# Attention keys stored block by block, constants in one transfer, stores spread over six blocks: a one-core attention and experts kernel

## The chip, the cores and the metric

The kernel runs on one core of a Trainium2 chip. The metric is the device time of one execution in microseconds (us); the number quoted for a kernel is the median of several runs. TensorE is called PE, its weight loads PEld, VectorE DVE, ScalarE ACT, GpSimd POOL and SyncE SP. SP does no arithmetic here: its queue issues nearly all transfers between the device's main memory and the on-chip memory. Those transfers are carried by 16 DMA engines.

## What is computed

Three layers follow each other. Attention has 8 heads over 4 sequences of 576 tokens; the first four heads see the last 32 keys, the other four see every fourth of the last 128. Its output, 2304 rows of 512, goes into a layer of 8 experts, of which each row uses the one with the highest gate value, and then into a plain feed-forward layer with a squared ReLU.

```python
scores = scale * np.matmul(q, k.transpose(0, 1, 3, 2))
mask_plain = (rel >= 0) & (rel < window)
mask_dil = (rel >= 0) & (rel < window * dilation) & (rel % dilation == 0)
...
attn = attn / (np.sum(attn, axis=-1, keepdims=True) + 1e-09)
return np.matmul(attn, v).astype(np.float32)
...
logits = x @ w_gate
e_idx = np.argmax(logits, axis=1)
...
eom = 1.0 / (1.0 + np.exp(-(x @ w_output_gate)))
for e in range(E):
    mask = e_idx == e
    h = np.maximum(x[mask] @ w1[e], 0.0)
    ye = h @ w2[e]
    out[mask] = gate_w[mask, None] * eom[mask, e, None] * ye
...
h = np.maximum(x @ w_in, 0.0)
return (h * h @ w_out).astype(np.float32)
```

## The kernel before

The 2304 tokens are cut into 18 blocks of 128. The attention stage is a loop over blocks 0 to 14 (`EARLY` is 15), written out by hand and software-pipelined: turn i transposes the probabilities of block i (`tr`), forms the scores of block i+2 (`qk`, L423 to L436), transposes the output of block i-1 (`xt`) and multiplies block i's probabilities by its values (`pv`). After the loop come blocks 15 to 17 with the last two groups of routing, and with them the start of the experts: once the most frequent expert is known (`choose`, its number in `e0_t`, L205), its first weights are loaded (`load_w(0, 0)`, L722), its list of tokens (`meta_load`, L723), and its rows are gathered from main memory (`gather(0)`, L725), where the attention stage has stored them in `x_d`. `gather(0)` reads rows of blocks 0 to 14 and so waits until all of these are stored. The first expert matrix product is L820.

Keys, queries and values are loaded in turn by SP. `load_k(i, n)` (L349) brings the keys of n blocks with two transfers into a ring of five blocks plus one that repeats the fifth for the wrap (`wrap`, L354). Before, the tile `kz` holds the four pairs of heads one after the other and within a pair the blocks, so a row of a load comes in four pieces of 512 bytes times n. `load_q` (L342) and `load_v` (L360) bring two blocks each, with rows of 4096 and 8320 bytes. `load_consts` (L401) issues six small transfers in turn 0, ahead of the values of blocks 4 and 5. `clear` (L411) sets the experts' lists in main memory to an empty mark in turn 3, with four transfers of 128 rows of 640 bytes.

`store(a, 2)` (L508) writes two blocks of attention output to `x_d` with three transfers: one for the 256 columns of the plain heads (L512), and one for each block's other 256 columns (L514), whose rows are put in another order on the way. `STORES` (L35) says in which turn a pair is stored: pairs 0 and 2 in turn 12, 4 to 8 in turn 13, 10 and 12 in turn 14; block 14 follows after the loop (L700).

The order of each engine's instructions is the order in which the program writes them. SP works through its queue in that order, so an instruction that waits holds up all behind it. Two kinds of waits matter: for an engine to be done with a buffer that a load overwrites, and for one of eight semaphores that SP's transfers use in turn, so that a transfer waits until the eighth before it has landed.

Of the kernel before, what the change touches and what calls it, by code (L numbers as in the profile page):

```python
# [10 lines left out]
F32 = mybir.dt.float32  # L11
F32R = mybir.dt.float32r
BF16 = mybir.dt.bfloat16
I32 = mybir.dt.int32
# [8 lines left out]
B, H, S, D = 4, 8, 576, 64  # L23
P = 128
NT = B * S
NB = NT // P

LAP = 5
# [15 lines left out]
MS = NT + 256  # L44
# [10 lines left out]
VL = -(-2 * VN // 128) * 128  # L55
VR = 6


# [8 lines left out]
@with_exitstack  # L67
def attention_experts_kernel(ctx: ExitStack, tc: tile.TileContext, qB, kB, vB, wg, wE, wF, consts, rows, ids, out):
    nc = tc.nc
# [14 lines left out]
    ones = cpool.tile([P, P], BF16, name="ones")  # L84
    w8 = cpool.tile([P, 4, E], F32, name="w8")
    eoff = cpool.tile([P, 4, E], F32, name="eoff")
    idsb = cpool.tile([P, NG, 4, 4], I32, name="idsb")
    wg_sb = cpool.tile([P, 4, 32], F32, name="wg_sb")
    cum = cpool.tile([P, NG + 1, E], BF16, name="cum")
# [233 lines left out]
    def attention():  # L323
# [6 lines left out]
        masks = c2.tile([P, 4, 2, 64], F32, name="masks")  # L330
        tri32 = c2.tile([P, P], F32, name="tri32")
        kz = c2.tile([P, 2, 4, (LAP + 1) * P], F32, name="kz")
        vb = c2.tile([P, 2, VR, 4, 4, D + 1], F32, name="vb")
# [15 lines left out]
        def load_k(i, n, engine=nc.sync):  # L349
            t = i % LAP  # L350
            for h2 in range(2):
                engine.dma_start(out=kz[h2:P:2, h2, :, P * (t + 1):P * (t + 1 + n)], in_=kB[h2, :, :, P * i:P * (i + n)])

        def wrap():  # L354

            o = LAP * P
            nc.scalar.copy(out=kz[:, :, 0:2, 96:P], in_=kz[:, :, 0:2, o + 96:o + P])
            nc.scalar.copy(out=kz[:, :, 2:4, 0:P], in_=kz[:, :, 2:4, o:o + P])

# [8 lines left out]
        def clear_k(t, first, second):  # L368
            first.memset(kz[:, 0, :, P * t:P * t + P], 0.0)
            second.memset(kz[:, 1, :, P * t:P * t + P], 0.0)  # L370

# [6 lines left out]
        o = 2 * P  # L378
# [3 lines left out]
        warm(8)  # L382
        nc.vector.memset(kz[:, :, 0:2, 96:P], 0.0)
        nc.vector.memset(kz[:, :, 2:4, 0:P], 0.0)
        load_q(1, 1)
# [15 lines left out]
        def load_consts():  # L401
            nc.sync.dma_start(out=wg_sb, in_=wg)
            nc.sync.dma_start(out=tri32, in_=consts[:, P:2 * P])
            nc.sync.dma_start(out=w8.rearrange("p a e -> p (a e)"), in_=consts[:, o + 512:o + 544])
            nc.sync.dma_start(out=eoff.rearrange("p a e -> p (a e)"), in_=consts[:, o + 544:o + 576])
            nc.sync.dma_start(out=idsb.rearrange("p a b c -> p (a b c)"), in_=ids)
            nc.sync.dma_start(out=rowc, in_=rows)

        z = stg.tile([P, DM], F32, tag="xg", name="zm", bufs=4).bitcast(I32)[:, 0:MS * E * 4 // P // 4].rearrange("p (n c) -> p n c", c=4)

        def clear():  # L411
            for h in range(4):
                nc.sync.dma_start(out=meta_d[E * MS // 4 * h:E * MS // 4 * (h + 1)].rearrange("(p n) c -> p n c", p=P), in_=z)

# [8 lines left out]
        def qk_mm(i):  # L423
            t = i % LAP
            s = ps_s.tile([P, H, 64], F32, tag="s", name="s")
            q = q_t.pop(i)
            for p in range(4):
                for c in range(4):
                    if p < 2:
                        rhs = kz[:, :, p, P * (t + 1) + 32 * (c - 1):P * (t + 1) + 32 * (c + 1)]  # L430
                    else:
                        rhs = kz[:, :, p, P * t:P * (t + 2)].rearrange("p h (s c m) -> p h s c m", s=2, c=4)[:, :, :, c, :]
                    nc.tensor.matmul(
                        out=s[32 * c:32 * c + 32, 2 * p:2 * p + 2, :], lhsT=q[:, p, 32 * c:32 * c + 32], rhs=rhs, start=True, stop=True
                    )
            s_t[i] = s  # L436
# [212 lines left out]
        for i in range(EARLY):  # L649
# [3 lines left out]
            t = (i + 2) % LAP  # L653
# [6 lines left out]

            for a in STORES.get(i, ()):
                store(a, 2)
            if i % 2 == 0 and i + 6 < NB:
# [866 lines left out]
def _layout(inputs):  # L1530
# [22 lines left out]
    kd = dilated(k, 0, 32).reshape(NB, 2, 2, P, D).transpose(2, 4, 1, 0, 3).reshape(2, D, 2, NT)  # L1553
    kB = np.ascontiguousarray(np.concatenate([kp, kd], axis=2))
    one = np.concatenate([v, np.ones((H, NT, 1), f)], axis=2)
# [18 lines left out]
def _consts():  # L1574
# [21 lines left out]
    rows = np.concatenate([e, E - 1 - e, np.array(WIN, f), e * MS, lt.reshape(-1), np.arange(NSPILL, dtype=f)])[None]  # L1596
    return dict(consts=consts, rows=np.ascontiguousarray(rows), ids=np.ascontiguousarray(ids.reshape(P, -1)))

# [13 lines left out]
```

## Time and profile before

| what | value |
|---|---|
| median of 3 runs | 741.49 us (737.64 to 742.68) |
| the profiled execution | 742.68 us, its span 741.0 us |
| PE busy | 698.2 us, 94% of the span |
| DVE, ACT, POOL busy | 487.4, 327.2, 115.0 us |
| DMA | 136.90 MB, 185 GB/s on average |

The span begins with the first instruction that the profile shows and ends with the last; 1.7 us of the execution lie around it. The profiled execution is the slowest of the three, 1.2 us above the median. Up to about 110 us PE is idle a good part of the time; from about 125 us on it is busy nearly without a break. In the rows below "[idle before <-releaser]" is how long the engine sat idle ahead of the instruction and what ended that.

### The profile page before, as it was taken

How to read it: one execution, taken by the hardware profiler on the slowest of the kernel's cores; microseconds unless marked ns; L12 is line 12 of the kernel's file. 1: busy time of each engine (PE TensorE's matmuls, PEld its weight loads, DVE VectorE, ACT ScalarE, POOL GpSimd, SP SyncE). 2: the span in 40 equal slices, each digit the busy share in tenths (PEclk: the TensorE clock that was granted, in tenths of full speed). 3: DMA queues.
4: the chain of work that ended last, by engine and by line, in shares of the span. 5: the costliest groups of instructions: out<-in, count | busy, mean ns of one | idle time of the engine just before them, and what ended most of it. 6: DMA issues, size and time to landing. Idle time of an engine off the chain costs nothing. (4 is left out here: it accounts for less than half of the span.)

```text
span 741.0 us, 13894 instructions
## 1 busy us (share of the span) xinstructions
PE 698.2 (94%) x5227; PEld 633.4 (85%) x5227; DVE 487.4 (66%) x898; ACT 327.2 (44%) x601; POOL 115.0 (16%) x122
## 2 busy tenths in 40 slices
PE   6699748999999999999999999999999999999995
PEld 4566527999999999999999999999988888888884
DVE  7656644587465665687886977877889854445431
ACT  2334323464454555565655555556444431222120
POOL 6244423510101101004400000000000030003003
PEclk9999987999999999999999999999999999999998
DMA  8988464766547567675437555466565453325302
GB/s 265 318 253 249 154 186 156 216 207 227 191 152 225 189 194 249 211 221 167 161 134 256 188 192 199 139 238 231 192 218 183 150 166 113 106 95 182 100 29 88
DMA packets 67155, 136.90 MB, mean 185 GB/s; under 512 B 10857, under 2 KB 43498, under 8 KB 66058
## 3 DMA queue, kind: packets, MB, share of 16 engines
q1 hardware_dynamic: 57434, 120.09, 50.4%
q0 software_dynamic: 4176, 10.57, 4.2%
q10 hardware_dynamic: 5472, 5.29, 2.1%
q8 instruction: 43, 0.70, 0.4%
q14 instruction: 30, 0.25, 0.1%
HBM read 102.00 MB, written 33.96 MB: 183 GB/s over the span
## 5 line engine op out<-in xcount | busy, mean ns | idle before, releaser
L1386 DVE TENSOR_TENSOR slot_d<-gq,slot_d 128x768 fp32r<-128x768 f32 x48 | 45.9, 957 | 64.3 <-ACT slot_d L1384 63.3
L1384 ACT CAST slot_d<-gq 128x768 fp32r<-128x768 f32 x48 | 40.0, 835 | 97.7 <-PE op L1422 86.9
L1431 POOL DMA_INDIRECT out<-os,idc x18 | 19.8, 1099 | 353.2 <-DVE os L1430 348.3
L834 ACT ACTIVATE hh<-hp 128x240 fp32r<-128x240 f32 (+6 forms) x72 | 29.1, 407 | 40.1 <-PE hp L822 39.7
L159 POOL DMA_INDIRECT xg<-x_d,mt x23 | 24.7, 1074 | 141.6 <-PE xp L183 95.8
L1377 DVE SCALAR_TENSOR_TENSOR gq<-gq 128x768 f32<-128x768 f32 x48 | 45.6, 950 | 1.0 <-DMA gq<-g_d 1.0
L1421 PE MATMUL op<-slot_b,slot_d 128*128 128x512 f32 x108 | 42.0, 389 | 0.0
L1423 PE MATMUL op<-slot_a,slot_d 128*128 128x512 f32 x108 | 42.0, 389 | 0.0
L1422 PE MATMUL op<-slot_b,slot_d 128*128 128x512 f32 x108 | 42.0, 389 | 0.0
L1423 PE MATMUL op<-slot_b,slot_d 128*128 128x512 f32 x108 | 42.0, 389 | 0.0
L1421 PE MATMUL op<-slot_a,slot_d 128*128 128x512 f32 x108 | 42.0, 389 | 0.0
L1422 PE MATMUL op<-slot_a,slot_d 128*128 128x512 f32 x108 | 42.0, 389 | 0.0
L141 DVE TENSOR_TENSOR slot_d<-raw,slot_d 128x1024 fp32r<-128x1024 f32 x24 | 29.3, 1227 | 18.9 <-ACT slot_d L140 17.9
L835 DVE SCALAR_TENSOR_TENSOR hl<-hp,hh 128x240 fp32r<-128x240 f32 (+6 forms) x72 | 31.2, 443 | 15.0 <-ACT hh L834 14.9
L849 ACT COPY ys<-yp 128x240 f32<-128x240 f32 (+6 forms) x36 | 14.3, 396 | 47.7 <-PE yp L822 34.4
L141 DVE TENSOR_TENSOR slot_b<-raw,slot_b 128x1024 fp32r<-128x1024 f32 x20 | 24.3, 1225 | 13.0 <-ACT slot_b L140 13.0
L821 PE MATMUL yp<-hl,slot_b 128*128 128x240 f32 (+3 forms) x112 | 31.7, 283 | 0.4 <-DVE hl L835 0.4
L820 PE MATMUL yp<-hh,slot_b 128*128 128x240 f32 (+3 forms) x112 | 31.9, 285 | 0.0
L822 PE MATMUL yp<-hh,slot_b 128*128 128x240 f32 (+3 forms) x112 | 31.6, 282 | 0.0
L141 DVE TENSOR_TENSOR slot_a<-raw,slot_a 128x1024 fp32r<-128x1024 f32 x15 | 18.3, 1227 | 19.7 <-ACT slot_a L140 19.3
L820 PE MATMUL hp<-xh,slot_d 128*128 128x384 f32 (+3 forms) x96 | 29.7, 310 | 0.0
L821 PE MATMUL hp<-xl,slot_d 128*128 128x384 f32 (+3 forms) x96 | 29.7, 309 | 0.0
(323 smaller groups left out, 2303.6 us busy)
## 6 DMA issues: line engine op xcount, KB each, us to landing
raw<-in_wE SPq DMA_DIRECT2D x63, 512.0 KB
g_d<-cr SPq DMA_DIRECT2D x96, 192.0 KB
gq<-g_d SPq DMA_DIRECT2D x48, 384.0 KB
raw<-in_wF SPq DMA_DIRECT2D x32, 512.0 KB
vb<-in_vB SPq DMA_DIRECT2D x16, 520.0 KB
yr<-yT_d SPq DMA_DIRECT2D x16, 384.0 KB
q<-in_qB SPq DMA_DIRECT2D x8, 512.0 KB
x_d<-x SPq DMA_DIRECT2D x22, 128.0 KB
```

The costliest lines, as they stand in the source:

```text
L141: nc.vector.tensor_tensor(out=lo, in0=raw, in1=hi.bitcast(F32), op=ALU.subtract)
L820: nc.tensor.matmul(out=out, lhsT=wh, rhs=mh, start=first, stop=False, skip_group_check=shared)
L821: nc.tensor.matmul(out=out, lhsT=wh, rhs=ml, start=False, stop=False, skip_group_check=shared)
L822: nc.tensor.matmul(out=out, lhsT=wl, rhs=mh, start=False, stop=last, skip_group_check=shared)
L834: nc.scalar.activation(out=h[:, :n], in_=p[:, :n], func=ACTF.Relu)
L835: nc.vector.scalar_tensor_tensor(out=l[:, :n], in0=p[:, :n], scalar=0.0, in1=h[:, :n].bitcast(F32), op0=ALU.max, op1=ALU.subtract)
L1377: nc.vector.scalar_tensor_tensor(out=x, in0=x, scalar=0.0, in1=x, op0=ALU.max, op1=ALU.mult)
L1384: nc.scalar.copy(out=h, in_=x)
L1386: return lambda: nc.vector.tensor_tensor(out=l, in0=x, in1=h.bitcast(F32), op=ALU.subtract)
L1421: nc.tensor.matmul(out=o_t[j], lhsT=h[:, a], rhs=w[:, 0], start=f == 0, stop=False)
L1422: nc.tensor.matmul(out=o_t[j], lhsT=h[:, a], rhs=w[:, 1], start=False, stop=False)
L1423: nc.tensor.matmul(out=o_t[j], lhsT=l[:, a], rhs=w[:, 0], start=False, stop=f == 15)
```

## The change

Keys: the tile becomes `kf`, in which a block's four pairs lie side by side (512 elements a block), and the array in main memory is laid out the same way on the host, so a row of a load is one piece of 2048 bytes times n. A score product of the plain heads for the first quarter of a block reads two pieces of 32 columns, through a view of `kf` that needs some columns behind the ring. Constants: five arrays become one (`late`), 1664 bytes a row, so `load_consts` issues two transfers. List clearing: one transfer of 2560 bytes a row; the tile that holds the mark is four times as large and taken from another pool. Stores: the pairs are stored in turns 9 to 14, and in each turn behind the loads of values, where they stood ahead of the loads of queries.

```diff
-STORES = {12: (0, 2), 13: (4, 6, 8), 14: (10, 12)}
+STORES = {9: (0,), 10: (2,), 11: (4,), 12: (6,), 13: (8,), 14: (10, 12)}
...
-        kz = c2.tile([P, 2, 4, (LAP + 1) * P], F32, name="kz")
+        kf = c2.tile([P, 2, KW], F32, name="kf")
+        kz = kf[:, :, 0:(LAP + 1) * 4 * P].rearrange("p h (t a s) -> p h t a s", t=LAP + 1, a=4)
...
-                engine.dma_start(out=kz[h2:P:2, h2, :, P * (t + 1):P * (t + 1 + n)], in_=kB[h2, :, :, P * i:P * (i + n)])
+                engine.dma_start(out=kf[h2:P:2, h2, 4 * P * (t + 1):4 * P * (t + 1 + n)], in_=kB[h2, :, 4 * P * i:4 * P * (i + n)])
...
         def load_consts():
-            nc.sync.dma_start(out=wg_sb, in_=wg)
-            nc.sync.dma_start(out=tri32, in_=consts[:, P:2 * P])
-            nc.sync.dma_start(out=w8.rearrange("p a e -> p (a e)"), in_=consts[:, o + 512:o + 544])
-            nc.sync.dma_start(out=eoff.rearrange("p a e -> p (a e)"), in_=consts[:, o + 544:o + 576])
-            nc.sync.dma_start(out=idsb.rearrange("p a b c -> p (a b c)"), in_=ids)
+            nc.sync.dma_start(out=late_sb, in_=late)
             nc.sync.dma_start(out=rowc, in_=rows)
...
-        z = stg.tile([P, DM], F32, tag="xg", name="zm", bufs=4).bitcast(I32)[:, 0:MS * E * 4 // P // 4].rearrange("p (n c) -> p n c", c=4)
+        z = raw_tile().bitcast(I32)[:, 0:MS * E * 4 // P].rearrange("p (n c) -> p n c", c=4)
 
         def clear():
-            for h in range(4):
-                nc.sync.dma_start(out=meta_d[E * MS // 4 * h:E * MS // 4 * (h + 1)].rearrange("(p n) c -> p n c", p=P), in_=z)
+            nc.sync.dma_start(out=meta_d.rearrange("(p n) c -> p n c", p=P), in_=z)
...
-                    if p < 2:
-                        rhs = kz[:, :, p, P * (t + 1) + 32 * (c - 1):P * (t + 1) + 32 * (c + 1)]
+                    if p < 2 and c:
+                        rhs = kz[:, :, t + 1, p, 32 * (c - 1):32 * (c + 1)]
+                    elif p < 2:
+                        o = (4 * t + p) * P + 96
+                        rhs = kf[:, :, o:o + 2 * (3 * P + 32)].rearrange("p h (s m) -> p h s m", s=2)[:, :, :, 0:32]
                     else:
-                        rhs = kz[:, :, p, P * t:P * (t + 2)].rearrange("p h (s c m) -> p h s c m", s=2, c=4)[:, :, :, c, :]
+                        rhs = kz[:, :, t:t + 2, p, 32 * c:32 * c + 32]
...
-            for a in STORES.get(i, ()):
-                store(a, 2)
             if i % 2 == 0 and i + 6 < NB:
                 load_q(i + 6, 2)
...
                 load_v(i + VR - 1, 2)
+            for a in STORES.get(i, ()):
+                store(a, 2)
```

On SP, in turns 0 to 2, the queue before holds from the query load of turn 0 to the keys of blocks 7 to 9 these rows (`vb` is the tile of the values, `wg_sb` to `rowc` are the constants):

```order
L345 DMA q_256<-in_qB 128x1024
L402 DMA wg_sb_79<-in_wg 128x128
L403 DMA tri32_108<-in_consts 128x128
L404 DMA w8_76<-in_consts 128x32
L405 DMA eoff_77<-in_consts 128x32
L406 DMA idsb_78<-in_ids 128x96
L407 DMA rowc_82<-in_rows 1x128
L363 DMA vb_110<-in_vB 64x2080 x4
L352 DMA kz_109<-in_kB 64x4x384 x2
```

and now these:

```order
L348 DMA q_252<-in_qB 128x1024
L404 DMA late_sb_76<-in_late 128x416
L405 DMA rowc_79<-in_rows 1x128
L365 DMA vb_106<-in_vB 64x2080 x4
L355 DMA kf_105<-in_kB 64x1536 x2
```

Four transfers fewer stand ahead of the values and of the keys of blocks 7 to 9, and a row of the keys is one piece where it was four.

On SP, in turns 9 to 13, the queue before holds from the values of blocks 14 and 15 on (`x_285`, `x_422`, ... are the pairs of attention output, the first of them blocks 0 and 1):

```order
L363 DMA vb_110<-in_vB 64x2080 x2
L352 DMA kz_109<-in_kB 64x4x256 x2
L345 DMA q_1048<-in_qB 128x1024
L363 DMA vb_110<-in_vB 64x2080 x2
L352 DMA kz_109<-in_kB 64x4x128 x2
L512 DMA x_d_66<-x_285 128x2x256
L514 DMA x_d_66<-x_285 4x32x256 x2
L512 DMA x_d_66<-x_422 128x2x256
L514 DMA x_d_66<-x_422 4x32x256 x2
```

and now:

```order
L365 DMA vb_106<-in_vB 64x2080 x2
L512 DMA x_d_66<-x_277 128x2x256
L514 DMA x_d_66<-x_277 4x32x256 x2
L355 DMA kf_105<-in_kB 64x1024 x2
L348 DMA q_1040<-in_qB 128x1024
L512 DMA x_d_66<-x_414 128x2x256
L514 DMA x_d_66<-x_414 4x32x256 x2
L365 DMA vb_106<-in_vB 64x2080 x2
L512 DMA x_d_66<-x_579 128x2x256
L514 DMA x_d_66<-x_579 4x32x256 x2
L355 DMA kf_105<-in_kB 64x512 x2
```

Three pairs of stores now stand between the last loads, all three of them ahead of the keys of block 17, the last row here; the other pairs and block 14 follow it as before.

## Rows read from the trace of the kernel before

**Rows 1.** Windows: stretch, its length, busy us of the engines, granted PE clock, DMA share, GB/s.

```profile
20.00:30.00 10.00, 9.03 (x210) 7.18 (x202) 8.05 (x25) 5.80 (x15) 3.12 (x3) 1.00 0.84 265
...
35.00:40.00 5.00, 3.59 (x60) 2.91 (x64) 1.38 (x2) 0.57 (x2) 0.00 (x0) 0.66 1.03 394
...
60.00:70.00 10.00, 9.13 (x192) 6.73 (x192) 6.51 (x17) 3.71 (x10) 5.23 (x6) 1.00 0.93 240
75.00:95.00 20.00, 14.08 (x296) 9.63 (x286) 13.08 (x59) 6.76 (x18) 10.96 (x11) 1.00 0.47 147
...
105.00:117.00 12.00, 6.58 (x23) 2.90 (x22) 6.45 (x24) 3.13 (x7) 6.50 (x7) 0.50 0.67 220
117.00:121.00 4.00, 3.66 (x17) 3.66 (x18) 1.31 (x4) 0.83 (x3) 0.52 (x1) 0.50 0.07 20
121.00:125.00 4.00, 4.00 (x36) 4.00 (x36) 1.96 (x4) 1.82 (x4) 1.53 (x3) 0.97 0.03 1
125.00:724.00 599.00, 596.62 (x3597) 560.48 (x3597) 410.13 (x659) 282.65 (x497) 57.73 (x55) 1.00 0.55 179
```

**Rows 2.** Waits of PE, 20 to 98 us: total, times, longest, in us.

```profile
PE s L433 <- DMA kz<-in_kB: 4.4, 1, 4.4
```

**Rows 3.** Timeline (start us, us, engine, what), 17 to 27 us, constants and clearing of values.

```profile
17.99 0.56 SPq L402 DMA_DIRECT2D wg_sb<-in_wg  x1
18.07 0.93 DVE L373 MEMSET vb<- 128x1040 f32 x1 [0.16 <-issue]
...
22.20 0.33 SPq L406 DMA_DIRECT2D idsb<-in_ids  x1
...
23.58 3.02 SPq L363 DMA_DIRECT2D vb<-in_vB  x4
...
26.70 1.38 SPq L352 DMA_DIRECT2D kz<-in_kB  x2
```

**Rows 4.** Timeline, the score products of blocks 7 and 8.

```profile
36.41 1.94 PE L433 MATMUL s<-kz,q 128*32 128x128 f32 x32 [4.40 <-DMA kz<-in_kB]
...
40.93 1.08 PE L433 MATMUL s<-kz,q 128*32 128x128 f32 x32
```

**Rows 5.** DMA view, SP's queue: packets, MB, share of 16 engines, 10 to 15 us.

```profile
q1 hardware_dynamic: 1034, 1.76, 100.6%
```

**Rows 6.** The same, 15 to 20 us.

```profile
q1 hardware_dynamic: 501, 1.80, 95.6%
```

**Rows 7.** Timeline of SP, 57 to 101 us: values of blocks 14 and 15, stores, weights, list.

```profile
57.98 1.13 SPq L363 DMA_DIRECT2D vb<-in_vB  x2
...
70.20 0.55 SPq L512 DMA_DIRECT2D x_d<-x  x1
...
94.73 1.16 SPq L512 DMA_DIRECT2D x_d<-x  x1
...
97.78 0.59 SPq L133 DMA_DIRECT2D raw<-in_wE  x1
...
100.00 0.40 SPq L153 DMA_DIRECT2D mt<-meta_d  x1
```

**Rows 8.** Timeline, the score product of block 17 on PE.

```profile
81.20 1.08 PE L433 MATMUL s<-kz,q 128*32 128x128 f32 x32
```

**Rows 9.** Timeline, from the chosen expert to the first expert product, 94 to 118 us.

```profile
94.14 0.14 DVE L205 CAST e_t<-e 1x1 int32<-1x1 f32 x1
...
104.84 1.04 ACT L140 CAST slot_a<-raw 128x1024 fp32r<-128x1024 f32 x1 [6.25 <-DMA raw<-in_wE]
105.92 1.28 DVE L141 TENSOR_TENSOR slot_a<-raw,slot_a 128x1024 fp32r<-128x1024 f32 x1 [8.79 <-ACT slot_a L140]
105.94 1.05 POOL L159 DMA_INDIRECT xg<-x_d,mt  x1 [11.23 <-DMA x_d<-x]
...
108.71 0.19 PE L587 MATMUL rk<-oh,tri 128*128 128x32 bf16 x1 [7.86 <-DVE oh L578]
...
117.34 0.57 PE L820 MATMUL hp<-xh,slot_a 128*128 128x240 f32 x1 [1.35 <-issue]
```

More of the change, by code (lines that the diff above doesn't have):

```diff
@@ L56 @@
 VR = 6
+KW = (LAP + 1) * 4 * P + 3 * P
 LEFT = ["A11", "A12", "A22", "S1", "S2", "S3", "S4"]
@@ L67, in attention_experts_kernel @@
 @with_exitstack
-def attention_experts_kernel(ctx: ExitStack, tc: tile.TileContext, qB, kB, vB, wg, wE, wF, consts, rows, ids, out):
+def attention_experts_kernel(ctx: ExitStack, tc: tile.TileContext, qB, kB, vB, wE, wF, consts, late, rows, out):
     nc = tc.nc
@@ L84, in attention_experts_kernel @@
     ones = cpool.tile([P, P], BF16, name="ones")
[L85 to L88, printed above, removed]
+    late_sb = cpool.tile([P, 2 * P + 8 * E + NG * 16], F32, name="late_sb")
+    wg_sb = late_sb[:, 0:P].rearrange("p (k e) -> p k e", k=4)
+    tri32 = late_sb[:, P:2 * P]
+    w8 = late_sb[:, 2 * P:2 * P + 4 * E].rearrange("p (a e) -> p a e", e=E)
+    eoff = late_sb[:, 2 * P + 4 * E:2 * P + 8 * E].rearrange("p (a e) -> p a e", e=E)
+    idsb = late_sb[:, 2 * P + 8 * E:].bitcast(I32).rearrange("p (g b c) -> p g b c", b=4, c=4)
     cum = cpool.tile([P, NG + 1, E], BF16, name="cum")
@@ L330, in attention @@
         masks = c2.tile([P, 4, 2, 64], F32, name="masks")
-        tri32 = c2.tile([P, P], F32, name="tri32")
-        kz = c2.tile([P, 2, 4, (LAP + 1) * P], F32, name="kz")
+        kf = c2.tile([P, 2, KW], F32, name="kf")
+        kz = kf[:, :, 0:(LAP + 1) * 4 * P].rearrange("p h (t a s) -> p h t a s", t=LAP + 1, a=4)
         vb = c2.tile([P, 2, VR, 4, 4, D + 1], F32, name="vb")
@@ L351, in load_k @@
             for h2 in range(2):
-                engine.dma_start(out=kz[h2:P:2, h2, :, P * (t + 1):P * (t + 1 + n)], in_=kB[h2, :, :, P * i:P * (i + n)])
+                engine.dma_start(out=kf[h2:P:2, h2, 4 * P * (t + 1):4 * P * (t + 1 + n)], in_=kB[h2, :, 4 * P * i:4 * P * (i + n)])
         def wrap():
-            o = LAP * P
-            nc.scalar.copy(out=kz[:, :, 0:2, 96:P], in_=kz[:, :, 0:2, o + 96:o + P])
-            nc.scalar.copy(out=kz[:, :, 2:4, 0:P], in_=kz[:, :, 2:4, o:o + P])
+            nc.scalar.copy(out=kz[:, :, 0, 0:2, 96:P], in_=kz[:, :, LAP, 0:2, 96:P])
+            nc.scalar.copy(out=kz[:, :, 0, 2:4], in_=kz[:, :, LAP, 2:4])
         def load_v(i, n, engine=nc.sync):
@@ L368, in clear_k @@
         def clear_k(t, first, second):
-            first.memset(kz[:, 0, :, P * t:P * t + P], 0.0)
-            second.memset(kz[:, 1, :, P * t:P * t + P], 0.0)
+            first.memset(kz[:, 0, t], 0.0)
+            second.memset(kz[:, 1, t], 0.0)
         def clear_v(j, h2, engine):
@@ L382, in attention @@
         warm(8)
-        nc.vector.memset(kz[:, :, 0:2, 96:P], 0.0)
-        nc.vector.memset(kz[:, :, 2:4, 0:P], 0.0)
+        nc.vector.memset(kz[:, :, 0, 0:2, 96:P], 0.0)
+        nc.vector.memset(kz[:, :, 0, 2:4], 0.0)
         load_q(1, 1)
@@ L1553, in _layout @@
     kd = dilated(k, 0, 32).reshape(NB, 2, 2, P, D).transpose(2, 4, 1, 0, 3).reshape(2, D, 2, NT)
-    kB = np.ascontiguousarray(np.concatenate([kp, kd], axis=2))
+    kB = np.concatenate([kp, kd], axis=2).reshape(2, D, 4, NB, P).transpose(0, 1, 3, 2, 4)
+    kB = np.ascontiguousarray(kB.reshape(2, D, NB * 4 * P))
     one = np.concatenate([v, np.ones((H, NT, 1), f)], axis=2)
@@ L1596, in _consts @@
     rows = np.concatenate([e, E - 1 - e, np.array(WIN, f), e * MS, lt.reshape(-1), np.arange(NSPILL, dtype=f)])[None]
-    return dict(consts=consts, rows=np.ascontiguousarray(rows), ids=np.ascontiguousarray(ids.reshape(P, -1)))
+    o = 2 * P + 512
+    late = [consts[:, P:2 * P], consts[:, o:o + 8 * E], ids.reshape(P, -1).view(f)]
+    return dict(consts=consts, late=late, rows=np.ascontiguousarray(rows))
 def kernel(**inputs):
@@ L1605 @@
     arrays = {**_layout(inputs), **_consts()}
+    arrays["late"] = np.ascontiguousarray(np.concatenate([arrays.pop("wg").reshape(P, -1)] + arrays["late"], axis=1))
     aps = {n: nc.dram_tensor(f"in_{n}", a.shape, mybir.dt.from_np(a.dtype), kind="ExternalInput").ap() for n, a in arrays.items()}
```

## The prediction

> **What bounds the kernel now.** I read the windows by stage first [rows 1]. From 125 to 724 us PE is busy for 596.6 of 599.0 us at a granted clock of 1.00, so in that stretch nothing but PE's own work counts, and the change does not touch it. What the attention stage gains or loses up to the first expert product at 117.34 us [rows 9] is therefore carried to the end one for one. The stage before is not bound by one engine: DMA is at 0.84 to 1.03 of its time up to 70 us, and at 0.47 from 75 to 95 us while PE has gaps. So the question there is which transfer is late.
>
> Two are. The first shows in PE's waits: once, for 4.4 us, PE stands before the score product of block 7 for its keys [rows 2, 4]. The second shows in the timeline around 105 us [rows 9]: the gather of the first expert's rows waits for 11.23 us, the profile says for the stores to `x_d`; ACT waits 6.25 us for the first weights; and DVE, which stands behind ACT, releases PE's `rk` product only at 108.71 us, after 7.86 us of idle PE. SP's timeline tells why all three are late together [rows 7]: the stores begin at 70.20 us, the last is issued behind 94.73 us, and the weights and the list of tokens, issued at 97.78 and 100.00 us, come behind them.
>
> **The change part by part: the front.** Keys first. What a piece costs is read from two stretches in which DMA is full: 1034 packets with 1.76 MB took 100.6% of 16 times 5 us, which is 80.5 us [rows 5], and 501 with 1.80 MB took 95.6%, 76.5 us [rows 6]. Two equations give 10.4 ns a packet and 39.6 us a MB, on one DMA engine. A load of keys has 512 pieces before and 128 after, so it saves 384 x 10.4 ns / 16 = 0.25 us. Six loads (blocks 0, 1, 2, 3 to 4, 5 to 6, 7 to 9) lie up to the wait of block 7: 1.5 us. The packets' sizes vary in each stretch, so I allow 0 to 3 us for this term.
>
> Constants. The values of blocks 4 and 5 are issued at 23.58 us, behind six small transfers that began at 17.99 us, the last but one of them at 22.20 [rows 3]. The clearing that the values need ends at 18.07 + 0.93 = 19.0 us, so with two transfers in place of six SP can issue them at about 20 us. The engines cannot gain the whole 3.5 us: their share from 20 to 30 us is 0.84, so 1.6 us of idle time is there to be filled. Some 512 packets less give 512 x 10.4 ns / 16 = 0.3 us. I take 1.9 us, between 0 (if the transfers ahead are what is slow) and 3.5.
>
> Together block 7's keys come 3.4 us sooner, and of the 4.4 us of waiting 1.0 are left. The wait also lets the granted clock fall (0.66 from 35 to 40 us [rows 1], which is a mix of 1.2 and 2.4 GHz), and the score product behind it takes 1.94 us where the next takes 1.08 [rows 4]. With a wait of 1 us I count these 0.9 us as gained: 4.3 us for the front, bounds 0 and 5.3. The queries of block 8 and the values come right behind these keys in the queue and move with them, so I see no next wait that gives it back at once.
>
> The list clearing moves the same bytes and saves another 0.25 us, behind the keys of block 7: nothing. Its mark is 640 elements a row instead of 160, on POOL; DVE needs 0.93 us for 1040 [rows 3], so this costs at most that once, and I take 0 because it is done ahead of turn 0's chain. The score products keep their columns, the clearing and the wrap keep their elements: 0, with nothing else to pay for them.
>
> **The change part by part: the stores.** Seven pairs go from 70.20 to 94.73 us on SP, 3.5 us a pair, while the DMA engines are busy for 0.47 of the time [rows 1, 7]. So something narrower than all 16 engines holds them. From the first store to the gather at 105.94 us it takes 35.7 us, block 14, the last loads ahead and the weights behind included [rows 7, 9].
>
> Now the first pair follows the values issued at 57.98 us, which take SP 1.13 us [rows 7]: 59.1 us, less 4.3 us from the front, 54.8. The same 35.7 us follow, and in between come the loads of keys 15 and 16, queries 16 and 17, values 16 and 17 and key block 17, that is 2.4 MB. At 39.6 us a MB over 16 engines they take 5.9 us; at the 240 GB/s of the stretch from 60 to 70 us [rows 1] they take 9.8. The end comes at 96.4 to 100.3 us, 5.6 to 9.5 us sooner than 105.94.
>
> The other limit is the compute chain. The expert's number stands at 94.14 us and its weights are issued 3.64 us later [rows 7, 9]; that moves with the front, by 4.3 us, less what the loads of the last turns lose behind the stores. From issue to ACT the weights take 7.06 us, mostly standing in the stores' queue, and that shrinks too. I take 6.0 us for gather, weights and list together, near the low end, because both limits have to agree. Bounds: 1 (the front's gain lost again, the queue as long as before) and 10.
>
> The added cost is in what stands behind the stores on SP. Keys of block 17 are now behind three pairs, 3 x 3.5 = 10.5 us. PE asks for them at 81.20 us [rows 8], with the front's gain at 76.9. The queue from 54.8 us to them holds two transfers of values (1.04 MB, 2.6 us), 10.5 us of stores and 5.9 to 9.8 us of loads: 73.8 to 77.7 us. So they come 3 us early to 1 us late, plus the time from issue to the first byte. I expect a wait of 0 to 2 us there, which the gather does not feel while the queue of stores decides.
>
> A rule of the Trainium skill (DMA: Bandwidth & Descriptors, the section on why a DMA increments its semaphore by 16) bears on the share of 0.47: a transfer is spread over the largest number of engines, up to 16, that divides the slowest dimension of both sides. For the re-ordering stores, with 4 as slowest dimension, that is four engines, and every load has a quarter of its bytes on the same four. By this rule spreading gains only what these four leave idle among the last loads, so the sum lies nearer to the 1 us bound, if they leave nothing; the trace's share agrees with it, but shows no engine by itself.
>
> **The clock behind it.** From 105 to 121 us the granted clock is 0.50, 1.2 GHz; 17 products take 3.66 us, where 36 take 4.00 at 2.4 GHz [rows 1], so these alone lose 1.8 us, and the transposes ahead of them perhaps another 0.7. PE's gap of 7.86 us [rows 9] shrinks to about 5, as its end moves by 6 and its start by 2 to 4. But 4.4 us were enough to lower the clock at block 7, so I take 0.5 us of a possible 2.5.
>
> **Sum.** 6.0 + 0.5 = 6.5 us (the front is inside the 6.0: it moves both limits). The profiled execution took 742.68 us, so 736.2 by its own time; it lies 1.2 us above the median of 741.49, against which the change is measured, so I predict 735.0 us.
>
> **The rivals.**
> The queue is conserved. The stores' engines carry the same bytes before and after, and were not idle between 59 and 70 us, as the share of 0.93 says [rows 1]. Then the early stores only delay the loads, the queue ends where it did, and about 2 us are left: 739.5 (738 to 741). For it: 240 GB/s at a full share says that reading was slow then. Against it: full share means all engines, and 0.47 later means that most had room.
>
> The stores make the last keys late, and the kernel slower. Place: the score product of block 17 on PE. If the front gains nothing, PE asks for them at 81.2 us, the stores start at 59.1, and with reads slowed by the writes beside them the keys land at 88 instead of 78 to 82. PE then stands for 7 us; everything up to the expert's number stands behind it in PE's queue, and the weights are issued 7 us later with an empty queue ahead, which returns some 4. It decides once that wait is over about 4 us, each us more counts in full, and a lowered clock adds up to 2.5: 744.5 (742 to 750). Against it: the front has a wait to remove and little that stands against it.
>
> The gap closes. With 9 us or more from the queue and compute in step, PE's gap falls to 3 us or so, the clock stays up and its 2.5 us come on top: 730 (727 to 732.5). For it: both bounds above allow it. Against it: the chain of the expert's number moves by 4.3 us at most.
>
> **How the numbers follow.** Forecast (732.5 to 738) 0.52; queue conserved 0.22; gap closes 0.18; slower 0.08. About what a measurement here can tell is 1%, 7.4 us: faster means under 734.1, slower over 748.9. All of the third rival and about half of the forecast lie under 734.1: 0.43. Over 748.9 lie the far end of the slower rival and what I have not seen: 0.05. Within 1%: 0.52. The range of 8 in 10 goes from 728 (the middle of the closing gap's span, roughly) to 743 (into the slower case); the forecast's own is 732.5 to 738.
>
> **What would show it.** Right: PE's wait before block 7's score product under 2 us, and no fall of the clock there; first store near 55 us, none of SP's queue left with stores at the time of the expert's number; gather at 99 to 101 us; first expert product at 110 to 112 us. Wrong: a new wait of PE for keys at block 15 or 17 of more than 2 us; a gather behind 103 us; a PE gap of over 6 us before `rk`; or any difference from 125 us on beyond the shift.

## The result and the profile after

The changed kernel takes 734.37 us in the median of 6 runs (733.13 to 736.75), the kernel before 739.72 us in 6 runs beside them (737.64 to 742.68): a ratio of 0.9916, 95% interval 0.9892 to 0.9939. It was measured twice more, on two chips, beside the experiments: 737.95 us of 12 runs against 740.25, 0.9962 (0.9936 to 0.9987), and 736.61 us of 10 runs against 740.31, 0.9944 (0.9918 to 0.9971). The second estimate lies outside the first's interval and the first outside the second's. Weighted by the number of runs of the changed kernel the three give 0.9946, that is 4.0 us of 740. A ratio here is an estimate from all runs of both kernels, not the quotient of the two medians; by the medians the three gains are 5.4, 2.3 and 3.7 us. All differences below are read with that spread in mind.

| what | before | after |
|---|---|---|
| the profiled execution | 742.68 us | 733.13 us |
| its span | 741.0 us | 731.5 us |
| PE busy | 698.2 us, 94% | 696.5 us, 95% |
| DMA packets | 67155 | 62307 |

The two profiled executions are 9.55 us apart, more than twice the measured gain: that of before is the slowest of its six runs, that of after the fastest. So one must ask of every piece of these 9.55 us whether it belongs to the change.

The windows of the changed kernel, by stage; the columns are those of [rows 1]:

```profile
20.00:30.00 10.00, 9.04 (x218) 7.29 (x214) 8.38 (x25) 5.68 (x14) 3.13 (x3) 1.00 1.01 388
35.00:40.00 5.00, 4.77 (x107) 3.56 (x107) 3.20 (x8) 2.97 (x6) 4.34 (x5) 1.00 0.97 352
...
75.00:95.00 20.00, 16.09 (x260) 11.03 (x259) 11.74 (x56) 6.76 (x18) 7.96 (x8) 0.85 0.48 141
...
105.00:117.00 12.00, 10.34 (x72) 8.75 (x73) 5.13 (x13) 4.42 (x10) 4.48 (x5) 0.87 0.37 119
117.00:121.00 4.00, 4.00 (x38) 4.00 (x37) 3.59 (x8) 2.81 (x6) 3.05 (x2) 1.00 0.64 201
```

From 20 to 30 us the DMA engines now have no idle time left (1.01 for 0.84) and move 388 GB/s where they moved 265; from 35 to 40 us PE is busy for 4.77 us where it was for 3.59, at a full granted clock. From 75 to 95 us the DMA share is as low as before (0.48 for 0.47), though the stores now lie earlier.

PE's waits of the changed kernel from 20 to 110 us (total, times, longest), with the answers to [rows 2] and to the gap in [rows 9]:

```profile
PE rk L587 <- DVE oh L578: 6.5, 1, 6.5
...
PE s L433 <- DMA kf<-in_kB: 1.7, 3, 0.8
```

And the places of [rows 3, 4, 7 to 9] in its timeline:

```profile
17.14 0.55 SPq L404 DMA_DIRECT2D late_sb<-in_late  x1
17.74 0.37 SPq L405 DMA_DIRECT2D rowc<-in_rows  x1
19.38 2.40 SPq L365 DMA_DIRECT2D vb<-in_vB  x4
...
31.74 1.08 PE L433 MATMUL s<-kf,q 128*32 128x128 f32 x32 [0.27 <-DMA kf<-in_kB]
...
55.19 0.51 SPq L512 DMA_DIRECT2D x_d<-x  x1
...
78.54 1.08 PE L433 MATMUL s<-kf,q 128*32 128x128 f32 x32 [0.56 <-DMA kf<-in_kB]
...
90.41 1.10 SPq L136 DMA_DIRECT2D raw<-in_wE  x1
93.42 0.39 SPq L156 DMA_DIRECT2D mt<-meta_d  x1
...
98.04 1.04 ACT L143 CAST slot_a<-raw 128x1024 fp32r<-128x1024 f32 x1 [6.48 <-DMA raw<-in_wE]
99.05 1.05 POOL L162 DMA_INDIRECT xg<-x_d,mt  x1 [11.31 <-DMA x_d<-x]
101.84 0.19 PE L587 MATMUL rk<-oh,tri 128*128 128x32 bf16 x1 [6.51 <-DVE oh L578]
110.27 0.38 PE L820 MATMUL hp<-xh,slot_a 128*128 128x240 f32 x1 [1.53 <-DVE xl L178]
```

Values 4.2 us sooner, the score product of block 7 4.67 us sooner and with 0.27 us of waiting instead of 4.40, the first store 15.0 us sooner, the gather 6.89 us, the first expert product 7.07 us. That product takes 0.38 us instead of 0.57: it runs at the upper level of the clock. The remaining 2.4 us of the 9.5 by which the spans differ lie behind it, some 1.9 us of them, by estimate, in that clock: before, the first 17 products took 3.66 us [rows 1], and at the rate of 38 in 4.00 us they would take 1.8.

### The profile page after: what moved, and what is told of

Its sections match the earlier page's. It is cut to its first block, busy times and chain, and to the rows that moved or that the text cites. A ratio compares the mean times of both kernels' runs of the same rounds, so it can differ in the third digit from the quotient of the medians.

```text
span 731.5 us, 13885 instructions
## 1 busy us (share of the span) xinstructions
PE 696.5 (95%) x5227; PEld 633.6 (87%) x5227; DVE 488.0 (67%) x898; ACT 327.6 (45%) x601; POOL 116.5 (16%) x122
## 2 busy tenths in 40 slices
DMA packets 62307, 136.90 MB, mean 187 GB/s; under 512 B 10361, under 2 KB 37242, under 8 KB 61210
```

## The experiments

Each kernel was timed beside the kernel before on the same chip; the sets below are one chip each. For each, its profile gives the time at which the expert's number stands (`e_t`), the start of the first gather, the idle gap of PE ahead of `rk` after the last routing block, and the first expert product with its own duration (0.57 us at 1.2 GHz, 0.38 at 2.4). "Stall" is the longest time of over 3 us that ACT or DVE stood between 77 and 89 us for a release that the profile puts to no instruction; it is taken up below. All are read from the timeline, in us:

| kernel | ratio to before | e_t | stall | gather | gap | first product |
|---|---|---|---|---|---|---|
| before | 1 | 94.14 | 3.94 | 105.94 | 7.86 | 117.34 (0.57) |
| constants and clearing alone | 0.9947 (0.9926 to 0.9968) | 85.40 | none | 100.68 | 11.41 | 111.75 (0.38) |
| keys alone | 0.9966 (0.9945 to 0.9988) | 87.80 | none | 103.81 | 11.85 | 115.21 (0.38) |
| stores spread alone | 0.9980 (0.9955 to 1.0005) | 91.76 | none | 103.30 | 7.63 | 114.69 (0.57) |
| keys and constants, stores in old turns | 0.9950 (0.9927 to 0.9974) | 85.71 | none | 100.95 | 11.38 | 112.37 (0.57) |
| changed kernel, first | 0.9916 (0.9892 to 0.9939) | 87.17 | none | 99.05 | 6.51 | 110.27 (0.38) |
| changed kernel, second | 0.9962 (0.9936 to 0.9987) | 89.62 | 5.19 | 98.34 | 2.48 | 110.81 (0.57) |
| changed kernel, third | 0.9944 (0.9918 to 0.9971) | 90.81 | 5.30 | 98.17 | 2.31 | 109.60 (0.38) |
| changed, stores from turn 3 on | 0.9958 (0.9931 to 0.9985) | 92.31 | 3.64 | 101.18 | 3.53 | 112.31 (0.38) |
| changed, stores cut otherwise | 0.9928 (0.9903 to 0.9954) | 89.92 | 3.70 | 98.66 | 2.30 | 109.84 (0.38) |
| the same, stores in old turns | 0.9914 (0.9888 to 0.9941) | 88.44 | 3.70 | 97.74 | 2.42 | 108.27 (0.38) |
| the same again | 0.9912 (0.9883 to 0.9940) | 90.25 | 4.38 | 98.99 | 2.51 | 110.46 (0.38) |
| before, stores cut otherwise | 0.9963 (0.9937 to 0.9990) | 93.34 | 4.33 | 102.41 | 2.57 | 114.85 (0.57) |

The theory to test was the prediction's: the front makes PE earlier, the stores' narrow queue makes the gather earlier, and both are needed. The rivals: the queue is conserved, so that only the front counts; or the stores carry the gain alone.

### The change in parts

Keys and constants with the stores left where they were (the changed kernel less this part of the diff):

```diff
-STORES = {9: (0,), 10: (2,), 11: (4,), 12: (6,), 13: (8,), 14: (10, 12)}
+STORES = {12: (0, 2), 13: (4, 6, 8), 14: (10, 12)}
...
+            for a in STORES.get(i, ()):
+                store(a, 2)
             if i % 2 == 0 and i + 6 < NB:
                 load_q(i + 6, 2)
...
-            for a in STORES.get(i, ()):
-                store(a, 2)
```

> The changed kernel with the stores put back to turns 12 to 14, ahead of the query loads. Theory (two limits): the front's gain moves the compute chain and with it the turn in which the stores begin, so the queue of stores ends sooner too; gather near 101 us (before 105.94, changed 99.05), first expert product near 112.5 us (117.34 and 110.27), time about 0.6% under before. Rival (the queue is conserved, all the gain is the front's): gather at 99 to 99.5 us and the changed kernel's time, 0.8% under before. Rival (all the gain is the stores'): gather at 105 to 106, time as before.

The spread stores alone: the same lines the other way, in the kernel before.

> The kernel before with the stores in turns 9 to 14 behind the value loads, keys and constants as before. Theory: the queue of stores ends 3 to 5 us sooner than before while the compute chain does not move, so gather near 102.5 us, first expert product near 114 us, time about 0.4% under before, and PE waits for the keys of block 7 for 4.4 us as before. Rival (the queue is conserved): gather within 1 us of 105.94, time as before. Rival (late keys): PE waits over 4 us for the keys of block 17 and the time is over before.

The constants' one transfer and the clearing's one transfer alone, and the keys' layout alone, in the kernel before:

```diff
-            nc.sync.dma_start(out=wg_sb, in_=wg)
...
+            nc.sync.dma_start(out=late_sb, in_=late)
```

> The kernel before with the constants and the list clearing in one transfer each, keys and stores as before. Theory: the values of blocks 4 and 5 are issued near 20 us instead of 23.58; PE's wait for the keys of block 7 falls from 4.4 to about 2.5 us; time 0.2 to 0.4% under before. Rival (what is slow are the transfers ahead): wait 4 us or more, time as before. Rival (only the slots of SP's queue matter): wait under 1 us.

```diff
-                engine.dma_start(out=kz[h2:P:2, h2, :, P * (t + 1):P * (t + 1 + n)], in_=kB[h2, :, :, P * i:P * (i + n)])
+                engine.dma_start(out=kf[h2:P:2, h2, 4 * P * (t + 1):4 * P * (t + 1 + n)], in_=kB[h2, :, 4 * P * i:4 * P * (i + n)])
```

> The kernel before with the keys stored block by block, constants, clearing and stores as before. Theory: 0.25 us for each of six loads, so PE's wait for the keys of block 7 falls from 4.4 to about 2.9 us; time 0.2 to 0.3% under before. Rival (a load costs its bytes, not its packets): wait within 0.4 us of 4.4, time as before.

Measured on one chip, beside 34 runs of before with a median of 741.41 us: 737.29 (front), 738.95 (stores), 736.61 (constants), 738.65 us (keys). The constants alone gain what the whole front gains; the keys add nothing to them; the spread stores alone cannot be told from no change. The place of the gather in the kernel with keys and constants (100.95 us) and its first product (112.37) are where the theory had them, and not where either rival did. With the spread stores alone the gather moved by 2.6 us, between the theory's 3.4 and the rival's 1; but `e_t` moved by 2.4 us with it, and that profile lacks the stall that the one of before has.

The wait for block 7's keys shows the same split. In the timelines, first of the kernel with the constants alone:

```profile
17.99 0.35 SPq L404 DMA_DIRECT2D rowc<-in_rows  x1
18.70 3.75 SPq L364 DMA_DIRECT2D vb<-in_vB  x4
22.80 1.71 SPq L353 DMA_DIRECT2D kz<-in_kB  x2
...
25.19 0.42 SPq L409 DMA_DIRECT2D meta_d<-raw  x1
...
32.39 1.08 PE L429 MATMUL s<-kz,q 128*32 128x128 f32 x32
```

and then of the one with the keys alone:

```profile
34.76 1.82 PE L437 MATMUL s<-kf,q 128*32 128x128 f32 x32 [4.05 <-DMA kf<-in_kB]
```

With the constants as one transfer the wait is gone altogether, as the rival with the slots of SP's queue had it (the theory had 2.5 us left), block 7's product starts at 32.39 us (36.41 before [rows 4], 31.74 in the changed kernel), and the old layout of the keys stays. With the new layout alone the wait is 4.05 us, and in two kernels that leave keys and constants as they were it is 3.11 (spread stores) and 3.8 us (cut stores): the 4.05 are within what the unchanged load shows, and within the 0.4 us of the rival in which a load costs its bytes and not its packets. What the constants cost before stands in the queue of SP in the kernel before:

```profile
19.59 0.33 SPq L404 DMA_DIRECT2D w<-in_consts  x1
20.90 0.33 SPq L405 DMA_DIRECT2D eoff<-in_consts  x1
22.20 0.33 SPq L406 DMA_DIRECT2D idsb<-in_ids  x1
...
28.81 3.09 SPq L413 DMA_DIRECT2D meta_d<-zm  x4
```

Each of these three takes SP 0.33 us, and the second and third start 1.3 us after the one before. SP's own waits from 17 to 25 us tell what it stands for (total, times, longest):

```profile
SPq L406 <- DMA vb<-in_vB: 1.0, 1, 1.0
SPq L405 <- DMA vb<-in_vB: 1.0, 1, 1.0
```

It is the landing of earlier loads of values. In the trace, L405 and L406 wait for the same two semaphores that they raise themselves, last taken by the loads of values issued at 13.58 and 14.32 us. So this is the wait for one of the eight semaphores: a transfer, however small, takes one of them, and here it is not issued before the eighth ahead of it has landed. Everything behind in the queue stands with it. The four clearing transfers take SP 3.09 us, the single one 0.42.

That the keys alone still gain 2.8 us in the median (2.5 by the ratio) is not explained by this wait; the profile does not say where it comes from.

### What the early stores do to the end of the queue

With the stores in their old turns, in the kernel with keys and constants changed, the end of the attention stage reads:

```profile
64.56 1.51 SPq L512 DMA_DIRECT2D x_d<-x  x1
...
85.71 0.14 DVE L208 CAST e_t<-e 1x1 int32<-1x1 f32 x1
...
91.76 0.51 SPq L514 DMA_DIRECT2D x_d<-x  x1
...
93.35 0.39 SPq L136 DMA_DIRECT2D raw<-in_wE  x1
94.00 0.40 SPq L156 DMA_DIRECT2D mt<-meta_d  x1
...
100.95 1.05 POOL L162 DMA_INDIRECT xg<-x_d,mt  x1 [14.67 <-DMA x_d<-x]
103.74 0.19 PE L587 MATMUL rk<-oh,tri 128*128 128x32 bf16 x1 [11.38 <-DVE oh L578]
```

The expert's number stands 8.4 us sooner than before (3.9 of them are the stall in the profile of before, of which more below), but its weights are issued 7.6 us behind it, since SP issues stores up to 92.3 us, and the gather comes 15.2 us behind it; PE's gap grows to 11.38 us. So here the queue is the limit, as the theory says. With the stores spread (the changed kernel, three profiles) the gather comes at 98.2 to 99.1 us, 1.9 to 2.8 us sooner, and the last store ahead of the weights starts at 88.58, 86.18 and 85.89 us; but PE's work ends later, so that `e_t` moves from 85.71 to between 87.17 and 90.81.

The second measurement was made to see whether the first gain would return, and together with it the following kernels.

> The changed kernel once more, beside the next three on the same chip: 0.8 to 1.0% under before, gather near 99 us, first expert product near 110 us.

It did not return in full: 737.95 us. Two things differ in this profile from the first one of the same program. One is a stall of ACT and DVE near 82 us, which the profile cannot name ("remote" is a release that it can put to no instruction that ended just before):

```profile
77.31 0.66 PE L520 MATMUL xt<-ident,x 128*128 128x128 f32 x4
...
81.97 0.37 ACT L522 COPY xT<-xt 128x256 f32<-128x256 f32 x1 [5.19 <-remote]
...
82.33 0.69 DVE L447 TENSOR_TENSOR sm<-s,masks 128x512 f32<-128x512 f32 x1 [5.12 <-remote]
```

The other is the clock at the first expert product (0.57 us). The same sort of stall stands in the profile of before, which the prediction was made from, as 3.94 us ahead of DVE's L555 at 88.39 us:

```profile
88.39 0.25 DVE L555 STREAM_TRANSPOSE ls<-lg 128x64 f32<-128x64 f32 x1 [3.94 <-remote]
```

What they wait for is PE. In the trace, the semaphore that ACT's L522 and DVE's L447 wait for is one that only PE's instructions raise. In the second profile it rises at 81.89 and 81.95 us, 4.5 and 4.0 us after the recorded ends of the score product (77.38) and of the transposes above (77.97) that raise it; in the profile of before it rises at 88.36, 3.9 us after the recorded end of PE's routing product (84.44). Without a stall, in the first profile, it rises 0.02 to 0.05 us after such an end. Why PE's signal comes so late is not shown.

The stall is in 8 of the 13 profiles, in two of the three of the changed kernel, with 3.6 to 5.3 us between 77 and 89 us, and missing in the other five. PE is held up with it, and its last work ahead of `rk` ends later: all seven profiles with a gap under 4 us have the stall, the five without it have gaps of 6.51 to 11.85 us. So a short gap says as much of the stall as of the queue. Part of the 9.55 us between the profiles of before and after is not the change's, and `e_t` in the table has to be read with that: of the three changed kernels it is 87.17 without a stall, and 89.62 and 90.81 with one of 5.2 and 5.3 us.

Stores begun still earlier:

```diff
-STORES = {9: (0,), 10: (2,), 11: (4,), 12: (6,), 13: (8,), 14: (10, 12)}
+STORES = {3: (0,), 5: (2,), 7: (4,), 9: (6,), 11: (8,), 13: (10,), 14: (12,)}
```

> The changed kernel with each pair stored as soon as it may be (turns 3, 5, 7, 9, 11, 13, 14). Theory: the queue is short at the end, gather near 96 us less what PE loses before, but the first stores stand among loads for which DMA is full (share 0.99 from 30 to 40 us), so PE waits for keys, queries or values 2 to 5 us more than in the changed kernel, and the time is within 0.3% of it. Rival (more spread is better): no new wait over 1 us and 0.4% under the changed kernel.

737.54 us, the same as the changed kernel beside it (737.95). The gather came at 101.18 us, later than before this edit and not sooner: with a stall of 3.64 us in this profile and `e_t` at 92.31 us, the compute chain is the limit, 8.9 us ahead of the gather. SP issues the last store ahead of the weights at 80.86 us, long before that. PE's waits for keys came to 1.4 us where they are 2.0 in the changed kernel beside it, so the theory's price of 2 to 5 us was not paid, and its gather near 96 us did not come either; the rival's gain of 0.4% did not show. In this profile, making the queue earlier still gives nothing once the compute chain is the limit.

### The stores' width

The re-ordering stores (L514) write rows in an order in which the slowest dimension is 4. The same bytes can be cut by the residue of the row instead, four transfers of 32 partitions for a pair, with 32 as slowest dimension:

```diff
-            for n in range(m):
-                engine.dma_start(out=d[P * n:P * n + P, 256:512].rearrange("(j r) c -> r j c", r=4), in_=x[:, a + n, 256:512])
+            for r in range(4):
+                engine.dma_start(
+                    out=d[:, 256:512].rearrange("(n j r) c -> r j n c", n=m, r=4)[r], in_=x[32 * r:32 * r + 32, a:a + m, 256:512]
+                )
```

In the changed kernel, and in the one with keys and constants changed and the stores in their old turns:

> The changed kernel with the re-ordering stores cut by residue: for each pair four transfers of 32 partitions by 2 blocks instead of two of 128 partitions in four groups, so that the slowest dimension is 32 and not 4. Theory (four engines hold the stores): the stores' queue is gone when the expert's number stands; DMA share from 75 to 85 us is under 0.45 and SP issues a pair in about 2.8 us; weights are with ACT 3.5 us after their issue instead of 7; gather near 95 us, first expert product near 106 us, time 0.4% under the changed kernel. Rival (what holds the stores is their number or the writing itself): five transfers a pair instead of three make the queue longer, gather at 99 us or later, time as changed or over.

> As the last, but with the stores in turns 12 to 14 as before the change. Theory (four engines): without the narrow queue the turn of the stores matters little: gather within 1.5 us of the last kernel's, time within 0.3% of it. Rival (it is the spread that helps): gather 3 us or more behind the last kernel's.

734.27 and 733.79 us on the chip where the changed kernel takes 737.95: 3.7 and 4.2 us less. The rival, time as changed or over, is out.

What the cut does shows in stretches in which SP's queue holds stores and nothing else, first with uncut stores (keys and constants changed, old turns), then with cut ones (the same kernel with the cut; columns as in [rows 1]):

```profile
77.00:78.50 1.50, 1.33 (x28) 0.80 (x20) 1.34 (x13) 1.04 (x4) 1.08 (x2) 1.00 0.29 96
```

```profile
75.00:76.50 1.50, 1.50 (x36) 1.08 (x35) 1.43 (x5) 0.00 (x0) 0.87 (x1) 1.00 0.58 149
```

A share of 0.29 is 4.6 of 16 engines, and SP's queue alone has 0.276 of it, 4.4 engines; with the cut it is 9.3. The share of the DMA engines while stores go out did not fall, as the first expectation had it, but rose: from 75 to 85 us it is 0.60 and 0.73, where it is 0.49 in the changed kernel's first profile and 0.56 with the uncut stores in old turns. (With the cut alone in the kernel before it is 0.54 there, for 0.52, but 0.66 for 0.47 from 75 to 95 us.) The gather at 95 us did not come either (98.66 and 97.74). The end of the stage with the cut stores in their old turns:

```profile
64.92 0.53 SPq L512 DMA_DIRECT2D x_d<-x  x1
65.50 2.75 SPq L514 DMA_DIRECT2D x_d<-x  x4
...
88.30 1.84 SPq L514 DMA_DIRECT2D x_d<-x  x4
...
90.91 0.38 SPq L136 DMA_DIRECT2D raw<-in_wE  x1
93.05 0.41 SPq L156 DMA_DIRECT2D mt<-meta_d  x1
...
95.00 1.04 ACT L143 CAST slot_a<-raw 128x1024 fp32r<-128x1024 f32 x1 [0.87 <-DMA raw<-in_wE]
97.74 1.05 POOL L162 DMA_INDIRECT xg<-x_d,mt  x1 [8.72 <-DMA x_d<-x]
98.81 0.18 PE L589 MATMUL rk<-oh,tri 128*128 128x32 bf16 x1 [2.42 <-DVE m L576]
```

The first store stands at 64.92 us, as late as with uncut stores (64.56), and yet SP is through with the stores at 90.1 us instead of 92.3, and the gather is 3.2 us sooner, in a profile that has a stall of 3.70 us where the other has none. PE's gap is 2.42 us instead of 11.38; 4.9 us of this are that `rk` comes sooner (98.81 for 103.74), and 4.0 that PE's work ahead of it ends later, with the stall. The weights reach ACT 4.1 us behind their issue (90.91 to 95.00), and 5.8 us in the second profile of this kernel; with uncut stores in the old turns it took 6.5 to 7.1 us. The theory had 3.5 us for this and 2.8 us for a pair on SP; from the first store to that of block 14 SP takes 3.3 us a pair here and 3.5 uncut. With cut stores the turn in which they are issued makes no measurable difference (734.27 and 733.79 us, gathers 0.9 us apart), as the theory had it.

The last set asked what the front is worth once the stores are cut, with the cut alone in the kernel before, and measured the changed kernel a third time.

> The kernel before with nothing changed but the re-ordering stores, each pair cut into four transfers of 32 partitions, so that the slowest dimension is 32. Theory (the stores' few engines set the gather, the front only ends PE's work sooner): the pair takes about as long as in the two earlier kernels with this cut (3 to 4 us), the queue is done soon after the last store is issued, and the gather comes at 100 to 102 us against 105.94; PE's idle gap before rk shrinks from 7.9 to 3 to 5 us, since PE has not been made earlier; the wait for block 7's keys stays at 4 us; time about 736, ratio 0.994 to 0.996. Rival A (front and cut add up fully): the same cut on the changed front gave 0.991, the front alone 0.995, so the cut alone would be worth 0.996 and leave the gather at 103 us or later. Rival B (once the stores are cut, nothing of the front counts): ratio 0.991, as with the changed front.

> The changed kernel on the same chip as the kernel with only the cut stores, since its two ratios so far, 0.992 and 0.996, lie further apart than their intervals. If the sessions differ, its ratio falls between these here too and the cut kernels beside it keep their distance to it; if the first measurement was a chance of few runs, it is 0.996 again.

> The changed front with the cut stores in their old turns, beside the kernel with only the cut stores on the same chip: the difference between the two is what the front is worth once the stores are cut. Theory: about 2 to 3 us (0.991 against 0.995), as the expert's number comes that much sooner and the queue no longer hides it. Rival B: no difference. Against the changed kernel it is faster by 2 us or more in either case, if the four engines of the stores were the holder.

738.94, 736.61 and 735.09 us, before 740.31. The cut alone is worth 0.9963 in the kernel before (interval 0.9937 to 0.9990), 2.7 us by the ratio and 1.4 by the medians, a little less than the 0.994 to 0.996 expected. On the changed front it is the step from 0.9950 to 0.9914 or 0.9912, again some 2.7 us, but across chips. In the profile of the cut alone the keys' wait is unchanged and the gap before `rk` small, beside a stall of 4.33 us:

```profile
PE s L433 <- DMA kz<-in_kB: 3.8, 1, 3.8
...
PE rk L589 <- DVE oh L580: 2.6, 1, 2.6
```

So front and width add up, as rival A had it: 0.9950 times 0.9963 is 0.9913, and on this one chip the front is worth 3.9 us on top of the cut (738.94 to 735.09), where 2 to 3 were expected. The place of the gather, 102.41 us, lies between what the theory and the rival gave. Rival B's 0.991 lies outside the interval of the cut alone. The changed front with cut stores in old turns is the fastest kernel here, 0.9914 and 0.9912 of before in two sets; against the changed kernel it was faster by 4.2 us in one set and by 1.5 us in the other, and the second difference is too small to be told from none, where 2 us or more were expected. The third measurement of the changed kernel falls between the first two, but the distance to the cut kernel was not kept, so neither of the two explanations put ahead of it is settled.

## Why the prediction came out as it did, point by point

The forecast was 735.0 us; the first measurement is 734.37, all three together 0.9946 of before, which is 737.5 on the scale of 741.49. The sign is as forecast, and so is the time of the first measurement. That it lies within 0.6 us is partly luck: a gain of 6.5 us was forecast, and the three measurements together give 4.0. The reasons held only in part.

**The front: size right, split wrong.** Forecast were 4.3 us; block 7's product starts 4.67 us sooner in the changed kernel, and no wait over 0.85 us for keys is left up to block 15. But the 1.5 us from the keys' pieces are not seen in this wait (4.05 us with them alone), and the constants, for which 1.9 us were taken with a bound of 3.5, alone removed the whole 4.4. The step that failed is the cap, that the engines cannot gain the whole 3.5 us because only 1.6 us of that stretch were idle. The idle time did not limit the gain: the values moved up by 4.2 to 4.9 us, and the stretch then ran at 1.01. What counted as busy had carried few bytes: at the forecast's own 39.6 us a MB the 2.65 MB of that stretch (265 GB/s over 10 us) are an estimated 6.6 us of the 8.4 that the share gives. That values would be issued when their clearing ends, at about 20 us, was right (DVE's clearing ends at 19.36, the transfer starts at 19.38). The list clearing, taken as nothing, frees 2.7 us of SP behind these keys; it was not tried apart from the constants.

**The stores: position right, worth less.** First store forecast at 54.8, seen at 55.19; the end of the queue at 96.4 to 100.3, gather at 99 to 101 forecast, 98.2 to 99.1 seen. The 6.0 us for the gather became 6.89 in the first profile. That no stores are left on SP when the expert's number stands had been named as a sign of being right: in the first profile the last ahead of the weights starts 1.4 us behind `e_t`, in the other two 3.4 and 4.9 us ahead of it. What failed is to whom the gain belongs. The forecast took 6.0 us for queue and front together. Apart from each other, the front measures 0.9950 and the spread stores 0.9980, and the spread stores on top of the front 0.9950 against 0.9946: nothing that can be told. The rival in which the queue is conserved, with about 2 us left of the whole change, describes the stores better than the forecast did; it was too low for the front, which alone gains 4.1 us by the medians.

The reason stands in the table. Two chains end at the gather: the queue of stores, and the chain from `e_t`, which takes 7.4 to 9.3 us in the seven profiles whose gap is under 4 us. (In the third profile of the changed kernel SP waits 2.4 us of it for entries of the list to land in main memory before it loads the list, L156.) With the front alone the queue is late (15.2 us behind `e_t`). With the spread the gather comes 1.9 to 2.8 us sooner, and then the compute chain is nearly as late, or later where a stall hits. The forecast said that both limits have to agree, and took the low end for that; it did not see that the profile of before holds 3.94 us of unnamed stall in the second of them.

**The narrow stores.** The rule of the Trainium skill (DMA: Bandwidth & Descriptors, the section on why a DMA increments its semaphore by 16), four engines for a slowest dimension of 4, put the gain of spreading near the low bound. That agrees with the runs: stores alone kept 4.4 engines' worth of the DMA share busy, spreading alone gave no gain that can be told, and cutting the same bytes so that the slowest dimension is 32 gave 3.7 and 4.2 us against the changed kernel in one set and 2.7 us (by the ratio) against before in another. No view names the engines themselves.

**The last keys.** A wait of 0 to 2 us before block 17's product was forecast: 0.56, 1.63 and 0.98 us in the three profiles. The rival that makes the kernel slower by this wait is out.

**The clock.** The gap before `rk` was forecast at about 5 us and was 6.51, 2.48 and 2.31. "A gap of over 6 us" had been named as a sign against the forecast; the first profile shows one, in the fastest execution. The two short gaps go with the stall. So the gap is no measure of the gain. The credit of 0.5 us was too small in the first profile, which has the upper level at the first expert product and with it, by the estimate above, 1.9 us. And the rival of the closing gap fails at its own step: in the second profile the gap is 2.48 us and the clock is low all the same.

**Carried to the end one for one.** Nearly. From the first expert product to the end of the execution it is 625.3 us before, and 622.9, 627.1 and 623.5 in the three profiles of the changed kernel. That spread of 4 us is as large as the gain. A difference behind the attention stage had been named as a sign against the forecast; part of it is the clock at the first products, the rest is not explained.

## What to carry to other kernels

Small transfers ahead of a needed load can cost more than their bytes, where each takes one of a few semaphores and waits for an earlier transfer to land: look at the distance between their starts, and at what the queue waits for. Before moving a queue earlier, find out which of two chains comes second where they meet, and whether the transfers use all engines; changing their shape can be worth more than changing their turn. And where runs of one kernel spread by as much as the change may bring, a stall that the profile cannot name must be taken out of a profile before a sum is made from it.

## What the runs showed that was not expected

The clock at the start of the experts does not follow the length of the gap ahead. The windows of the kernel with the constants alone, whose gap is 11.41 us:

```profile
108.00:112.00 4.00, 2.46 (x11) 1.27 (x10) 1.61 (x4) 0.98 (x3) 2.65 (x3) 0.81 0.65 224
112.00:116.00 4.00, 4.00 (x37) 4.00 (x37) 1.23 (x4) 1.92 (x4) 0.43 (x1) 1.00 0.07 15
```

and those of the changed kernel in its second profile, with a gap of 2.48 us:

```profile
108.00:112.00 4.00, 2.65 (x11) 2.01 (x10) 1.54 (x4) 1.34 (x4) 0.86 (x1) 0.50 0.24 63
112.00:116.00 4.00, 4.00 (x27) 4.00 (x26) 0.42 (x2) 0.79 (x3) 0.77 (x1) 0.68 0.03 3
```

In the first the clock is back at the upper level when the products start, in the second it is low for part of the first products: 27 of them in 4 us instead of 37. Five of the 13 profiles start the experts at the lower level; from the first product to the end of the execution these take 624.5 to 627.1 us, the other eight 622.6 to 624.6. What sets the moment at which the clock falls and returns was not tried.

The other unexpected thing is the unnamed stall of 3.6 to 5.3 us between 77 and 89 us, which comes and goes between profiles of one program. It shows on ACT or DVE, or on both at once, and both wait for a signal of PE that comes late. What holds it up stays open, and so does why the first measurement of the changed kernel gained more than the second.
